# Retention, Mish layer and SwiGLU on one core: moving weight preparation from the retention steps into the slots behind them

## The chip, the cores and the metric

The kernel runs on one core of a Trainium2 chip. The time is the device time of one execution in microseconds, and the smaller it is the better. The kernel before takes 932.82 us (median of 3 runs, 932.62 to 933.05).

## What is computed

Three stages in float32, each feeding the next. The first is retention: causal scores with a decay per head, and no softmax. The second is a two-matrix layer with Mish. The third is a gated layer with SiLU (SwiGLU).

```python
# q, k, v: (4, 8, 576, 64)
scores = scale * q @ k.T ; ret = scores * Dmat      # Dmat[i, j] = gamma[h] ** (i - j), 0 above the diagonal
x = (ret @ v) -> (2304, 512)
h = x @ w_in                                        # (512, 2048)
x = (h * tanh(softplus(h))) @ w_out                 # (2048, 512)
out = (silu(x @ w_gate) * (x @ w_val)) @ w2_out     # 512 -> 1536 -> 512
```

## The kernel before

**Retention** is a list of 20 steps `t`, five for each of the four batches: 128 rows of the sequence each, the fifth of a batch 64 rows. A step has TensorE work (scores `s`, the transposes of k of step t+1 into `tk`, of q ahead of time into `tq`, the state, and the output `o` in two parts, L436 and L443), ScalarE copies (`kT`, `qT`, `sbd`), VectorE work (the mask product `p`, L385, two of them, and the scaled output into `x`, L456) and one GpSimd product `vs`. At its end SP issues the loads of q for step t+4 and of k and v for step t+3. The pools of k and v hold three tiles, so k of step t+3 can only be issued when the state of step t has read k of step t.

**The first layer** is cut into 384 columns of tokens and 16 blocks of 128 hidden units, which makes 96 slots `s` (L577). A slot multiplies block i of the layer's first matrix by x (`g1`, 12 matmuls into a PSUM tile `h`), takes Mish on ScalarE (`m`, L568), splits the result into a high part (ScalarE cast, L573) and a low part (VectorE subtract, L574), together `g`, and multiplies the `g` of four slots earlier by the second matrix (`g2`, 12 matmuls into `acc`, LAG = 4). A slot with i = 0 has `g2` ahead of `g1`. The tiles `h` come from four PSUM banks in turn, so `g1` of slot s+4 overwrites what Mish of slot s has read. Slot 0 stands behind the output of step 17, slot 1 ahead of the output of step 19, slots 2 and on behind retention.

**Weight units.** Both matrices are needed as a high and a low half. There are 32 units of 128 x 1024 words, in the order of `todo` (L67 to L73): four of the first matrix, then one of each in turn. A unit goes through a pipeline, one stage in each call of `weights` (L129): SP fetches it into one of four raw buffers (`fetch`, L83); two calls later ScalarE scales its high words (L103) and VectorE shifts its low ones (L104); one call later VectorE puts in the sign (L108) and joins the words (L112); and then ScalarE copies out the high half (L122) and GpSimd subtracts for the low one (L123), which frees the raw buffer. With `late` set, as in the slots, this last stage waits for the next call. So one call in full flow is one fetch, a scale and a copy on ScalarE, a sign, a shift and a join on VectorE (in this order) and a subtract on GpSimd. Every engine takes its instructions in the order of the program. "Call A" and "call B" below are the first and the second call in a slot. Slot s needs unit 2s - 4 for `g1` and unit 2s - 3 for `g2` (from slot 4 on); a loop in the slot runs further calls if too few are there.

Retention calls the pipeline once in every step (L499), the slots once each until all 32 units are there (L598).

Of the kernel before, what the change touches and what calls it, by code (L numbers as in the profile page):

```python
# [16 lines left out]
def retention_mish_swiglu(  # L17
# [28 lines left out]
    NA, NBU = 19, 13  # L46
# [26 lines left out]
    n1 = len(todo)  # L73
# [9 lines left out]
    def fetch(lim):  # L83
        j = stage[0]
        if j >= min(lim, len(todo)) or j - stage[3] >= RAW:
            return
        stage[0] += 1
        kind, i, src = todo[j]
        raw[j] = xp.tile([128, 2 * DM], U32, tag="raw", name=f"raw{j}", bufs=RAW)
        dst = raw[j] if kind in ("out", "fin") else raw[j].rearrange("p (k f) -> p k f", k=KT)  # L90
        nc.sync.dma_start(out=dst, in_=src)  # L91


    def rebias():
        j = stage[1]
        if j >= stage[0]:
            return
        stage[1] += 1
        rebias_raw(j)
# [6 lines left out]
    def sign(j):  # L106
        lo, hi = words(j)
        nc.vector.scalar_tensor_tensor(lo, hi, 0x80000000, lo, op0=ALU.bitwise_and, op1=ALU.bitwise_or)  # L108

    def join(j):  # L110
        lo, hi = words(j)
        nc.vector.scalar_tensor_tensor(lo, hi, 3, lo, op0=ALU.logical_shift_left, op1=ALU.bitwise_or)  # L112

    def part(lim):
        j = stage[3]
        if j >= min(lim, stage[2]):
            return
        stage[3] += 1
        kind, i, _ = todo[j]
        u = pools["a" if j < NA else "b"].tile([128, 2, DM], F32R, tag="u", name=f"u{j}")  # L120
        w = words(j)[0].bitcast(F32)
        nc.scalar.copy(out=u[:, 0, :], in_=w)  # L122
        nc.gpsimd.tensor_tensor(out=u[:, 1, :], in0=w, in1=u[:, 0, :].bitcast(F32), op=ALU.subtract)  # L123
        unit[kind, i] = u
# [4 lines left out]
    def weights(lim, late=False):  # L129
        j = stage[2]  # L130
        on = j < min(lim, stage[1])
        if on:
            sign(j)
        yield
        if late:
            part(lim)
        if stage[1] < seen[0]:
            rebias()
        seen[:] = seen[1], stage[0]
        yield  # L140
        if on:
            join(j)
            stage[2] += 1
        while not late and stage[3] < stage[2]:
            part(lim)
        fetch(lim + 3)
        seen[1] = stage[0]

    def run(step):
        for _ in step:  # L150
            pass
# [118 lines left out]
    def retention(slot):  # L270
        with ExitStack() as c0:
# [29 lines left out]
            def load(t):  # L301
                if t >= len(steps):
                    return
                b, sc, n = steps[t]
                for nm, src in (("k", k), ("v", v)):
                    x = ld.tile([128, H, D], F32, tag=nm, name=f"{nm}{t}")
                    nc.sync.dma_start(
                        out=x[:n], in_=src[b, :, sc * 128:sc * 128 + n, :].rearrange("h p d -> p h d")
                    )
                    qkv[nm, t] = x  # L310
# [30 lines left out]
            def q_ahead(t, half):  # L341
                b, sc, n = steps[t]
                due = (
                    ((b, 1, 0),) if b else (),
                    ((b, 1, 1),) if b else ((b, 1, 0), (b, 1, 1)),
                    ((b, 2, 0),),
                    ((b + 1, 0, 0),),
                    ((b + 1, 0, 1),),
                )[sc]
                if half < len(due):  # L350
                    q_transposes(*due[half])

            def transposes(t):
                if t >= len(steps):
                    return
                b, sc, n = steps[t]
                src = qkv["k", t]
                p = ps1.tile([128, NP, 128], F32, tag="tk", name=f"tk{t}")
                for pr in range(NP):
                    nc.tensor.transpose(p[:, pr, :n], src[:n, 2 * pr:2 * pr + 2, :], ident[:n, :n])  # L360
                kT[t] = at.tile([128, NP, 128], F32, tag="kT", name=f"kT{t}")
                nc.scalar.copy(out=kT[t][:, :, :n], in_=p[:, :, :n])
                vs[t] = at.tile([128, H, D], F32, tag="vs", name=f"vs{t}")
                nc.gpsimd.tensor_tensor(  # L364
                    out=vs[t][:n],
                    in0=qkv["v", t][:n],
                    in1=gv[:n, sc, :].unsqueeze(2).to_broadcast([n, H, D]),
                    op=ALU.mult,
                )

            def scores(t):
                b, sc, n = steps[t]
                s = [ps1.tile([128, NP, 128], F32, tag=f"s{e}", name=f"s{e}_{t}") for e in range(2)]
                for pr in range(NP):
                    for e in range(2):
                        nc.tensor.matmul(  # L376
                            s[e][:n, pr, :n],
                            lhsT=kT[t][64 * e:64 * e + 64, pr, :n],
                            rhs=q_cols(t)[64 * e:64 * e + 64, pr],
                            start=True,  # L380
                            stop=True,
                        )
                pp[t] = [at.tile([128, NP, 128], F32, tag=f"p{e}", name=f"p{e}_{t}") for e in range(2)]
                for e in range(2):
                    nc.vector.tensor_tensor(  # L385
                        out=pp[t][e][:n, :, :n],
                        in0=s[e][:n, :, :n],
                        in1=mask[:n, :n].unsqueeze(1).to_broadcast([n, NP, n]),
                        op=ALU.mult,
                    )  # L390


            def gout_chunk(sc):
                nc.gpsimd.tensor_tensor(
                    out=gout[:, :, sc * 128:sc * 128 + 128],
                    in0=gout[:, :, :128],
                    in1=gstep[:, :, sc:sc + 1].to_broadcast([128, NP, 128]),
                    op=ALU.mult,
                )
# [3 lines left out]
            def state(t):  # L403
                b, sc, n = steps[t]
                if sc == nsc - 1:
                    return
                if sc == 0:
                    stp[b] = ps1.tile([128, NP, D], F32, tag="st", name=f"state{b}")
                for pr in range(NP):
                    for e in range(2):  # L410
                        h = 2 * pr + e
                        nc.tensor.matmul(  # L412
                            stp[b][64 * e:64 * e + 64, pr, :],
                            lhsT=qkv["k", t][:n, h, :],
                            rhs=vs[t][:n, h, :],
                            start=(sc == 0 and pr == 0),
                            stop=(sc == nsc - 2),
                            skip_group_check=True,
                        )
# [73 lines left out]
            for t in range(len(steps)):  # L493
                scores(t)
                transposes(t + 1)
                q_ahead(t, 0)
                state(t)
                q_ahead(t, 1)
                run(weights(NA))  # L499
                if t + 1 < nsc:  # L500
                    gout_chunk(t + 1)
                if t == len(steps) - 1:
                    slot(1)
                output(t)
                if t == len(steps) - 3:
                    slot(0)
                load_q(t + 4)
                load(t + 3)

    with tc.manual_schedule():  # L510
# [66 lines left out]
        def slot(s):  # L577
            b, i = divmod(s, F1)
            if i == 0 and s:
                g2(s - LAG)  # L580
            g1(s)
            if s >= LAG and i:
                g2(s - LAG)
            d, nm, j = xt, "x", b + 1
            parts = () if b + 1 == NB else (i - F1 + 4,) if b and F1 - 4 <= i < F1 - 2 else range(2, KT) if i == F1 - 1 else ()
            mish(s)
            for kk in parts:
                split_hi(d, nm, j, kk)
            halves(ws.pop(s), s)
            if s < F1 + OFF:  # L590
                while not parts and stage[3] < min(2 * s - OFF + 2 if s > OFF else s, n1):
                    run(weights(n1))
            for kk in parts:
                split_lo(d, nm, j, kk, nc.vector)
            if s >= LAG:
                g2_out(s - LAG)
            if s < F1 + OFF and not parts:
                run(weights(n1, True))  # L598
            second(s)

        retention(slot)
# [282 lines left out]
```

## Time and profile before

| | |
|---|---|
| median of the runs shown | 932.82 us |
| the profiled execution | 934.33 us |
| its span | 932.5 us |
| TensorE busy | 912.3 us, 98% |
| VectorE, ScalarE, GpSimd busy | 520.2, 362.3, 108.6 us |
| granted TensorE clock, mean | 1.00 |

The profiled execution is 1.5 us above the median and 1.8 us above its span. The page of the profile gives busy times and groups of instructions; the stretches show where an engine has idle time; the list of waits shows what ended it; the rows in order of time show what stands behind what. An instruction that is blocked on its engine shows as a longer one.

### The profile page before, as it was taken

The page shows a single profiled execution, that of the slowest core. Times are in us where ns is not written, and L with a number is a line of the kernel's source. Part 1 is how long each engine was busy: PE and PEld are TensorE (multiplying, and loading weights), DVE is VectorE, ACT ScalarE, POOL GpSimd, SP SyncE. Part 2 cuts the span into 40 slices and gives each one's busy share as a digit, 9 for nine tenths or more (in the row PEclk, how much of TensorE's full clock was granted, in tenths as well). Part 3 has the DMA queues.
Part 4 walks back from the last instruction along what each step waited for, and adds up shares of the span by engine and source line. Part 5 has one row for each costly group of instructions (what it writes and reads, how often), then busy time and mean ns, then how long its engine had stood idle before and what let it go on. Part 6 is the DMA issues. An engine that isn't in the chain of part 4 may idle for free.

```text
span 932.5 us, 14692 instructions
## 1 busy us (share of the span) xinstructions
PE 912.3 (98%) x5684; PEld 867.8 (93%) x5684; DVE 520.2 (56%) x929; ACT 362.3 (39%) x731; POOL 108.6 (12%) x90
## 2 busy tenths in 40 slices
PE   8888999999999999999999999999999999999998
PEld 7777899999999999999999999998999998999997
DVE  3897797246556565656535444556544556544444
ACT  4776564345444554545434222223222223222222
POOL 3775344000000000000000000000000000000000
PEclk9999999999999999999999999999999999999999
DMA  9999554035354463554554855544644444644421
GB/s 227 249 236 258 146 152 132 1 113 192 127 185 143 142 201 117 166 182 138 175 180 176 296 203 203 203 158 158 226 158 158 158 158 158 226 158 158 158 69 68
DMA packets 115351, 156.58 MB, mean 168 GB/s; under 512 B 45393, under 2 KB 80977, under 8 KB 115281
## 3 DMA queue, kind: packets, MB, share of 16 engines
q1 hardware_dynamic: 114176, 155.21, 53.4%
q8 instruction: 45, 0.74, 0.4%
q10 hardware_dynamic: 1104, 0.42, 0.2%
q14 instruction: 26, 0.20, 0.1%
HBM read 122.58 MB, written 33.03 MB: 167 GB/s over the span
## 4 chain that ended last, share of the span: by engine, by line
PE 88%; DMA 5%; DVE 3%; ACT 2%; SPq 1%; issue 1%; POOL 0%; ACTq 0%; DVEq 0%; POOLq 0%
PE t L777 28%; PE acc L551 20%; PE h L517 20%; PE fa L703 16%; DMA k<-in_k_dram 4%; PE o L436 1%; PE o L443 1%; DMA rawg<-in_moe_w_gate_dram 1%; PE tk L360 1%; PE s L376 1%; PE state L412 0%; DMA comb<-c 0%; DMA q<-in_q_dram 0%; SPq L91 0%; DVE p L385 0%
## 5 line engine op out<-in xcount | busy, mean ns | idle before, releaser
L777 PE MATMUL t<-y,su 128*128 128x384 f32 x1512 | 306.5, 338 | 1.0 <-DVE cv L744 1.0
L777 PEld LDWEIGHTS t<-y,su 128*128 128x128 f32 x1512 | 271.4, 188 | 24.4 <-DVE cv L744 2.3
L551 PE MATMUL acc<-g,u 128*128 128x384 f32 x1152 | 214.6, 336 | 0.9 <-ACT y L561 0.9
L517 PE MATMUL h<-xs,u 128*128 128x384 f32 x1152 | 214.6, 336 | 0.0
L551 PEld LDWEIGHTS acc<-g,u 128*128 128x128 f32 x1152 | 201.3, 188 | 1.5 <-ACT y L561 1.2
L517 PEld LDWEIGHTS h<-xs,u 128*128 128x128 f32 x1152 | 200.9, 188 | 0.3 <-issue 0.2
L703 PE MATMUL fa<-fu,g 128*128 128x512 f32 x648 | 190.0, 395 | 0.1
L703 PEld LDWEIGHTS fa<-fu,g 128*128 128x128 f32 x648 | 118.6, 188 | 7.5 <-ACT g L725 0.5
L574 DVE TENSOR_TENSOR g<-m,g 128x384 fp32r<-128x384 f32 x96 | 53.6, 558 | 126.8 <-ACT g L573 126.4
L725 ACT CAST g<-sg 128x384 fp32r<-128x384 f32 x72 | 36.9, 513 | 175.0 <-DVE sg L762 121.4
L568 ACT ACTIVATE m<-h 128x384 f32<-128x384 f32 x96 | 47.0, 490 | 145.4 <-PE h L517 144.3
L751 ACT ACTIVATE sg<-sg 128x384 f32<-128x384 f32 x54 | 28.4, 525 | 96.4 <-DVE sg L744 96.4
L730 DVE TENSOR_TENSOR g<-sg,g 128x384 fp32r<-128x384 f32 x72 | 40.2, 558 | 40.6 <-ACT g L725 40.6
L177 POOL TENSOR_TENSOR f<-rawf,f 128x256 fp32r<-128x256 f32 x24 | 23.4, 992 | 284.3 <-ACT f L176 284.3
L123 POOL TENSOR_TENSOR u<-raw,u 128x512 fp32r<-128x512 f32 x32 | 47.1, 1473 | 62.7 <-ACT u L122 61.4
L573 ACT CAST g<-m 128x384 fp32r<-128x384 f32 x96 | 49.3, 514 | 2.6
L744 DVE TENSOR_TENSOR u<-t,p 128x384 f32<-128x384 f32 x36 | 20.1, 557 | 49.8 <-PE t L777 45.6
L744 DVE TENSOR_TENSOR v<-t,p 128x384 f32<-128x384 f32 x36 | 20.0, 556 | 38.1 <-PE t L777 37.4
L104 DVE TENSOR_SCALAR raw<-raw 128x512 uint32<-128x512 uint32 x32 | 36.7, 1146 | 0.0
L762 DVE TENSOR_TENSOR sg<-sg,cv 128x384 f32<-128x384 f32 x54 | 30.2, 559 | 1.9
L122 ACT CAST u<-raw 128x512 fp32r<-128x512 f32 x32 | 21.2, 663 | 20.7 <-DVE raw L112 20.7
L364 POOL TENSOR_TENSOR vs<-v,gv 128x512 f32<-128x512 f32 (+1 forms) x20 | 26.3, 1313 | 22.5 <-DMA v<-in_v_dram 13.2
(79 smaller groups left out, 742.7 us busy)
## 6 DMA issues: line engine op xcount, KB each, us to landing
su<-comb SPq DMA_DIRECT2D x126, 512.0 KB, 3.3
comb<-c SPq DMA_DIRECT2D x84, 256.0 KB, 4.0
raw<-in_moe_w_in_dram SPq DMA_DIRECT2D x16, 512.0 KB, 5.8
raw<-in_moe_w_out_dram SPq DMA_DIRECT2D x16, 512.0 KB, 3.7
rawg<-in_moe_w_gate_dram SPq DMA_DIRECT2D x12, 512.0 KB, 6.5
rawf<-in_moe_w_out_dram SPq DMA_DIRECT2D x12, 512.0 KB, 4.5
rawv<-in_moe_w_val_dram SPq DMA_DIRECT2D x12, 512.0 KB, 6.2
find<-f SPq DMA_DIRECT2D x24, 256.0 KB, 2.4
```

The costliest lines, as they stand in the source:

```text
L104: nc.vector.tensor_scalar(lo, lo, 29, None, op0=ALU.logical_shift_right)
L123: nc.gpsimd.tensor_tensor(out=u[:, 1, :], in0=w, in1=u[:, 0, :].bitcast(F32), op=ALU.subtract)
L517: nc.tensor.matmul(ps, lhsT=u[:, a, kk * 128:(kk + 1) * 128], rhs=s[:, e, :], start=(c == 0), stop=(c == n - 1),)
L551: nc.tensor.matmul(accs[b][d][:, :T], lhsT=u[:, a, d * 128:(d + 1) * 128], rhs=g[:, e, :], start=(i == 0 and c == 0), stop=(i == F1 - 1 an ...
L568: nc.scalar.activation(w, hs.pop(s), AF.Mish)
L573: nc.scalar.copy(out=g[:, 0, :], in_=x)
L574: nc.vector.tensor_tensor(out=g[:, 1, :], in0=x, in1=g[:, 0, :].bitcast(F32), op=ALU.subtract)
L703: nc.tensor.matmul(accs["f", b][m], lhsT=gs[u, e, h][:, x, m * 128:(m + 1) * 128], rhs=fu[2 * (u % PAIRS) + e][:, a, :], start=first, stop ...
L725: nc.scalar.copy(out=gs[u, e, h][:, 0, :], in_=x)
L730: nc.vector.tensor_tensor(out=g[:, 1, :], in0=x, in1=g[:, 0, :].bitcast(F32), op=ALU.subtract)
L744: nc.vector.tensor_tensor(out=out_, in0=a, in1=b_, op=ALU.add)
L777: nc.tensor.matmul(p, lhsT=w[:, n % 2, a, kk * 128:(kk + 1) * 128], rhs=y[:, x, kk, :], start=begin and kk == 0 and (a, x) == (0, 0), stop ...
```

## The change

In retention the call of the pipeline is kept in steps with an odd number only, so there are 10 calls in place of 20. In each slot that still needs units, the call at its end is made twice. Nothing else changes; TensorE's instructions and their order are the same.

```diff
--- before.py
+++ after.py
@@ -496,7 +496,8 @@
                 q_ahead(t, 0)
                 state(t)
                 q_ahead(t, 1)
-                run(weights(NA))
+                if t % 2:
+                    run(weights(NA))
                 if t + 1 < nsc:
                     gout_chunk(t + 1)
                 if t == len(steps) - 1:
@@ -595,7 +596,8 @@
             if s >= LAG:
                 g2_out(s - LAG)
             if s < F1 + OFF and not parts:
-                run(weights(n1, True))
+                for _ in range(2):
+                    run(weights(n1, True))
             second(s)
 
         retention(slot)
```

VectorE, at slot 0 between steps 17 and 18. `x5` is the output of step 17, `g0` the low part of slot 0, `p0_18` and `p1_18` the masked scores of step 18, and the number behind `raw` is that of the unit. Before:

```order
L456 TENSOR_TENSOR x5_1344<-o17_1397,gout_146 128x4x128
L574 TENSOR_TENSOR g0_1428<-m0_1426,g0_1428 128x384
L108 SCALAR_TENSOR_TENSOR raw15_1261<-raw15_1261 128x512
L104 TENSOR_SCALAR raw16_1326<-raw16_1326 128x512
L112 SCALAR_TENSOR_TENSOR raw15_1261<-raw15_1261 128x512
L385 TENSOR_TENSOR p0_18_1447<-s0_18_1437,mask_144 128x512
L385 TENSOR_TENSOR p1_18_1448<-s1_18_1438,mask_144 128x512
```

and now:

```order
L456 TENSOR_TENSOR x5_1263<-o17_1316,gout_146 128x4x128
L575 TENSOR_TENSOR g0_1347<-m0_1345,g0_1347 128x384
L108 SCALAR_TENSOR_TENSOR raw6_1069<-raw6_1069 128x512
L104 TENSOR_SCALAR raw7_1189<-raw7_1189 128x512
L112 SCALAR_TENSOR_TENSOR raw6_1069<-raw6_1069 128x512
L108 SCALAR_TENSOR_TENSOR raw7_1189<-raw7_1189 128x512
L104 TENSOR_SCALAR raw8_1314<-raw8_1314 128x512
L112 SCALAR_TENSOR_TENSOR raw7_1189<-raw7_1189 128x512
L385 TENSOR_TENSOR p0_18_1375<-s0_18_1365,mask_144 128x512
L385 TENSOR_TENSOR p1_18_1376<-s1_18_1366,mask_144 128x512
```

A second sign, shift and join stand between `g0` and the masked scores of step 18, and the units in them are nine lower in number.

VectorE, slots 2 and 3, right behind retention (`g2`, `g3` and `g4` are the low parts of slots 2, 3 and 4). Before:

```order
L574 TENSOR_TENSOR g2_1589<-m2_1587,g2_1589 128x384
L108 SCALAR_TENSOR_TENSOR raw19_1478<-raw19_1478 128x512
L104 TENSOR_SCALAR raw20_1517<-raw20_1517 128x512
L112 SCALAR_TENSOR_TENSOR raw19_1478<-raw19_1478 128x512
L574 TENSOR_TENSOR g3_1616<-m3_1614,g3_1616 128x384
L108 SCALAR_TENSOR_TENSOR raw20_1517<-raw20_1517 128x512
L104 TENSOR_SCALAR raw21_1541<-raw21_1541 128x512
L112 SCALAR_TENSOR_TENSOR raw20_1517<-raw20_1517 128x512
L574 TENSOR_TENSOR g4_1659<-m4_1657,g4_1659 128x384
```

and now:

```order
L575 TENSOR_TENSOR g2_1517<-m2_1515,g2_1517 128x384
L108 SCALAR_TENSOR_TENSOR raw11_1436<-raw11_1436 128x512
L104 TENSOR_SCALAR raw12_1460<-raw12_1460 128x512
L112 SCALAR_TENSOR_TENSOR raw11_1436<-raw11_1436 128x512
L108 SCALAR_TENSOR_TENSOR raw12_1460<-raw12_1460 128x512
L104 TENSOR_SCALAR raw13_1469<-raw13_1469 128x512
L112 SCALAR_TENSOR_TENSOR raw12_1460<-raw12_1460 128x512
L575 TENSOR_TENSOR g3_1553<-m3_1551,g3_1553 128x384
L108 SCALAR_TENSOR_TENSOR raw13_1469<-raw13_1469 128x512
L104 TENSOR_SCALAR raw14_1527<-raw14_1527 128x512
L112 SCALAR_TENSOR_TENSOR raw13_1469<-raw13_1469 128x512
L108 SCALAR_TENSOR_TENSOR raw14_1527<-raw14_1527 128x512
```

Between the low parts of two slots there are six instructions of the pipeline in place of three. This goes on to slot 11; slot 12 has one sign and one join, and from slot 13 on there are none.

SP's queue, from step 9's loads on (the number behind k and v is the step that they are for). Before:

```order
L91 DMA raw9_862<-in_moe_w_out_dram 128x1024
L307 DMA k12_878<-in_k_dram 128x8x64
L307 DMA v12_880<-in_v_dram 128x8x64
L91 DMA raw10_929<-in_moe_w_in_dram 128x4x256
L298 DMA q14_944<-in_q_dram 64x8x64
L307 DMA k13_946<-in_k_dram 128x8x64
L307 DMA v13_948<-in_v_dram 128x8x64
L91 DMA raw11_995<-in_moe_w_out_dram 128x1024
L292 DMA q15_1013<-in_q_dram 128x8x128
```

and now:

```order
L307 DMA k12_833<-in_k_dram 128x8x64
L307 DMA v12_835<-in_v_dram 128x8x64
L298 DMA q14_890<-in_q_dram 64x8x64
L307 DMA k13_892<-in_k_dram 128x8x64
L307 DMA v13_894<-in_v_dram 128x8x64
L91 DMA raw5_941<-in_moe_w_out_dram 128x1024
L292 DMA q15_959<-in_q_dram 128x8x128
L307 DMA k14_961<-in_k_dram 64x8x64
L307 DMA v14_963<-in_v_dram 64x8x64
```

A fetch stands in every second step only, and the loads behind steps 8, 10, 12 and so on follow one another with no fetch between.

## Rows read from the trace of the kernel before

**Rows 1.** Page, part 1: busy us (share of the span) x instructions.

```profile
PE 912.3 (98%) x5684; PEld 867.8 (93%) x5684; DVE 520.2 (56%) x929; ACT 362.3 (39%) x731; POOL 108.6 (12%) x90
```

**Rows 2.** Stretches: steps 2 to 17; retention's end to slot 16.

```profile
core 0: us, PE busy (x) PEld busy (x) DVE busy (x) ACT busy (x) POOL busy (x), PEclk, DMA share, GB/s
...
19.46:99.31 79.85, 70.10 (x954) 60.08 (x953) 68.03 (x96) 55.61 (x107) 50.86 (x38) 1.00 1.05 247
...
111.47:165.86 54.39, 54.39 (x317) 54.39 (x314) 44.63 (x59) 31.47 (x59) 22.50 (x14) 1.00 0.44 136
```

**Rows 3.** Waits, 19.46 to 99.31: us in total, times, longest.

```profile
PE tk L360 <- DMA k<-in_k_dram: 7.4, 7, 2.0
...
PE state L412 <- ACT sbd L426: 1.7, 2, 1.1
...
PE o L443 <- DVE p L385: 0.4, 2, 0.2
```

**Rows 4.** Waits of SP's queue, the same stretch.

```profile
SPq L91 <- POOL u L123: 10.3, 7, 3.2
```

**Rows 5.** Order of time, slot 0 to step 18: start, us, engine, line, instruction.

```profile
103.24 0.69 DVE L108 SCALAR_TENSOR_TENSOR raw<-raw 128x512 uint32<-128x512 uint32 x1
...
103.84 0.42 DVE L104 TENSOR_SCALAR raw<-raw 128x512 uint32<-128x512 uint32 x1
104.18 0.68 DVE L112 SCALAR_TENSOR_TENSOR raw<-raw 128x512 uint32<-128x512 uint32 x1
104.78 1.28 DVE L385 TENSOR_TENSOR p<-s,mask 128x512 f32<-128x512 f32 x2
...
105.52 0.43 PE L443 MATMUL o<-p,vs 128*64 128x128 f32 x2 [0.83 <-DVE p L385]
105.63 1.29 POOL L123 TENSOR_TENSOR u<-raw,u 128x512 fp32r<-128x512 f32 x1 [3.36 <-ACT u L122]
```

**Rows 6.** Order of time, one slot with one call.

```profile
122.25 0.68 DVE L112 SCALAR_TENSOR_TENSOR raw<-raw 128x512 uint32<-128x512 uint32 x1
122.85 0.55 DVE L574 TENSOR_TENSOR g<-m,g 128x384 fp32r<-128x384 f32 x1
122.96 0.66 ACT L122 CAST u<-raw 128x512 fp32r<-128x512 f32 x1 [0.97 <-DVE raw L112]
123.31 0.68 DVE L108 SCALAR_TENSOR_TENSOR raw<-raw 128x512 uint32<-128x512 uint32 x1
...
123.70 1.48 POOL L123 TENSOR_TENSOR u<-raw,u 128x512 fp32r<-128x512 f32 x1 [1.66 <-ACT u L122]
...
123.92 1.54 DVE L104 TENSOR_SCALAR raw<-raw 128x512 uint32<-128x512 uint32 x1
...
124.61 0.52 ACT L573 CAST g<-m 128x384 fp32r<-128x384 f32 x1
...
125.38 0.68 DVE L112 SCALAR_TENSOR_TENSOR raw<-raw 128x512 uint32<-128x512 uint32 x1
```

**Rows 7.** VectorE and GpSimd in order of time, where a join meets a GpSimd product.

```profile
62.67 0.68 DVE L112 SCALAR_TENSOR_TENSOR raw<-raw 128x512 uint32<-128x512 uint32 x1
62.69 1.56 POOL L364 TENSOR_TENSOR vs<-v,gv 128x512 f32<-128x512 f32 x1 [0.83 <-PE tk L360]
...
87.26 0.42 DVE L104 TENSOR_SCALAR raw<-raw 128x512 uint32<-128x512 uint32 x1
87.27 1.30 POOL L364 TENSOR_TENSOR vs<-v,gv 128x512 f32<-128x512 f32 x1 [0.48 <-DMA v<-in_v_dram]
...
87.59 1.53 DVE L112 SCALAR_TENSOR_TENSOR raw<-raw 128x512 uint32<-128x512 uint32 x1
```

**Rows 8.** VectorE in order of time: the low part of slot 2.

```profile
116.58 0.54 DVE L574 TENSOR_TENSOR g<-m,g 128x384 fp32r<-128x384 f32 x1
```

**Rows 9.** Chain that ended last: the last product of slot 15 and the first of slot 16.

```profile
163.78 4.16 PE acc L551 x24
```

**Rows 10.** DMA issues, 118 to 136 us: count, KB each, median us to landing.

```profile
raw<-in_moe_w_in_dram SPq DMA_DIRECT2D x3, 512.0 KB, 3.7
```

## The prediction

> **What bounds the kernel now.** The page comes first: TensorE is busy for 98% of the span [rows 1], so a change counts only where it takes TensorE's idle time away or makes new. The stretches say where that idle time is [rows 2]. In steps 2 to 17 TensorE works 70.10 of 79.85 us. From 111.47 (the start of slot 2; I call it R, the end of retention) to 165.86 (the start of slot 16) it works all of 54.39 us. So there is something to win in retention, 9.75 us, and in the slots only something to lose. The list of waits names the 9.75 us [rows 3]: 7.4 for k from memory, 1.7 for ScalarE's copy of the state behind a copy of the pipeline, 0.4 for a mask product: 9.5. The DMA engines are full there, a share of 1.05 at 247 GB/s [rows 2], and SP stands 10.3 us before fetches until GpSimd frees a raw buffer, with the next loads of k and v queued behind [rows 4]. TensorE's order does not change, so the sum has three terms: what retention wins, what slot 0 costs it, and the idle time that the slots get.
>
> **Term 1, half of retention's calls go.** Up to step 17 there are 9 fetches in place of 18. That is 9 x 0.52 = 4.7 MB of 79.85 us x 247 GB/s = 19.7 MB [rows 2]. The other 15.0 MB take 61 us at this rate, less than TensorE's 70.10, so memory no longer sets the pace. Behind even steps no fetch stands before the loads, and a raw buffer is free long before its next fetch. VectorE and ScalarE lose a sign, shift, join, scale and copy in these steps, GpSimd a subtract; they ran beside TensorE and count only through the 2.1 us of waits for them. Of the 9.5 us I take 8.2 as gone: the loads of k that follow half a megabyte of q, and one wait for the state's copy in an odd step, may keep about 1.3. The ends are half of it, 4.8, and all of it, 9.5.
>
> **How VectorE and GpSimd meet.** This sets the other two terms. A free shift takes 0.42 us and a free sign or join 0.68 [rows 5]. One that comes while a GpSimd instruction runs ends only behind it: the shift at 123.92 takes 1.54 and ends 0.28 after the subtract [rows 6], the join at 87.59 takes 1.53 and ends 0.55 after the product. Who comes first wins: the join at 62.67, 0.02 ahead of the product, takes its 0.68, and the product is the longer one, 1.56 against 1.30 [rows 7].
>
> **Term 2, the second call in slot 0.** It stands ahead of step 18's mask products, for which TensorE waits already (0.83) [rows 5]. Its sign takes the place of the product, at 104.78. By the spacing of the same three rows the shift follows 0.60 later and the join would start 0.34 after that, at 105.72. The subtract comes at 105.63, under the shift, and goes first, as at 87.27 [rows 7]; it runs from about 105.69 for 1.29, and the join ends 0.55 later, at 107.53. Without the call VectorE was free at 104.86. So the products come 2.7 us later, and so does all of TensorE's work up to R. With the join first it would be 0.60 + 0.34 + 0.60 = 1.5.
>
> **Term 3, two calls in slots 2 to 11.** One slot with one call [rows 6], from join to join: the join ends at 122.93, the copy starts 0.03 later, the subtract at 123.70 and ends at 125.18, the shift ends at 125.46, the next join at 126.06: 3.13 us, a closed loop over three engines, in which the low part (0.55) and the sign are hidden. Call A is this same loop, 3.13. In call B no low part stands ahead. With a for the end of A's join, the sign starts at a - 0.08, the shift at a + 0.52, and the join would at a + 0.86. The subtract of the unit joined by A comes at a + 0.77 (122.93 to 123.70), 0.09 sooner. It runs from the shift's end, a + 0.83, to a + 2.13, and the join ends at a + 2.68. So a slot takes 3.13 + 2.68 = 5.8 us on this loop, against TensorE's 4.16 (two products in 4.16) [rows 9]. ScalarE needs less, so its added scales and copies are hidden there. A fetch goes out when B's subtract frees a buffer, at a + 2.13, and lands 3.7 us later [rows 10], at a + 5.8; the shift of the next slot's B wants it at a + 5.8 + 0.5. That fits with half a us to spare, and SP holds nothing else back, only further fetches.
>
> TensorE has a lead of four slots, and this is what hides the loop at first. The low part of slot 2 ends at 117.12 now, R + 5.65 [rows 8]. With a call more before it and one less ahead of step 19's products I put R + 6.1; the bounds are 5.1 and 8.3. Ten slots on, the low part of slot 12 ends at R + 6.1 + 58.1 = R + 64.2. Slot 16 opens with the product that reads it, at R + 54.4 [rows 2, 9]. So TensorE stands 9.8 us in sum. It begins about slot 11 or 12, where `g1` waits for a PSUM bank that Mish of four slots before has not read yet, with some 1.65 us a slot. From slot 13 on no calls are left and the low parts follow their products; nothing later has idle time that could give the loss back.
>
> **Sum.** -8.2 + 2.7 + 9.8 = +4.3 us. The profiled execution's 934.33 becomes 938.6, its span 936.8. The median of the runs shown is 1.5 lower: 932.8 + 4.3 = **937.1 us**. With term 1 between 9.5 and 4.8 this case goes from 935.8 to 940.5.
>
> **Rivals.**
> *Call B's join gets in first.* It misses by 0.09 us by my spacing, and a copy that starts late would turn it. Then ScalarE's order sets the loop: from a copy's start to the end of its cast 2.17 us [rows 6], then the low part and sign (about 1.1), the subtract 1.29, 0.28 for the shift and 0.60 for the join: about 5.45. Slot 12's low part ends at R + 5.1 + 54.5 = R + 59.6, an idle time of 5.2, and slot 0 costs 1.5: -8.2 + 1.5 + 5.2 = -1.5, 931.3 us (930.0 to 934.7 with term 1's ends).
> The Trainium skill (SBUF — State Buffer, section Who interferes with whom) says that VectorE instructions with two SBUF inputs share a port pair with GpSimd, that the first to start keeps it for the whole instruction, and that the order of issue decides. By that rule alone either order is possible, 937.1 or 931.3; the rows at 87.27 are what makes me choose.
> *The lead is never used up: faster.* If the two engines met less than rows 6 show, a slot would be 0.55 + 2 x 1.54 = 3.6 us of VectorE, under 4.16, and TensorE would not stand at all: -8.2 + 1.5 = -6.7, 926.1 us. It decides at about 4.85 us a slot, where slot 12 is just in time. Against it: the single loop is 3.13, so call B would have to do with 1.7.
> *Everything blocks.* Call B as long as A, 6.26 a slot, the late start R + 8.3, and half of term 1: -4.8 + 2.7 + (8.3 + 62.6 - 54.4 = 16.5) = +14.4, 947.2 us. A fetch that lands late would do the same.
> *The clock.* The wait ahead of step 18's output grows from 0.83 to 3.5 us; the longest now is 2.0 [rows 3], and the granted clock stays at 1.00, its level of 2.4 GHz [rows 2]. If it fell to 1.2 GHz behind this wait, the 5.9 us of work from 105.52 to R could take twice as long: up to 943.0 us.
> The Trainium skill (TensorE: The Clock Gate, section HAM oscillation — how this bites in real kernels) warns of long idle gaps for this reason; no row here shows a lower clock.
>
> **How the numbers follow.** The forecast gets 0.52, the join first 0.22, the lead that holds 0.12, everything blocked 0.09, the clock 0.05. 930.0 to 943.0 leaves out the third and most of the fourth, 0.2. Faster by over 0.2% (1.9 us, about what a measurement of this kernel can tell from no change) are the third case and a third of the second, 0.20; within 0.2% the rest of the second and the edge of the forecast, 0.16; slower 0.64.
>
> **What would show it.** Right: waits for k in steps 2 to 17 near 1 us; R near 106 (111.47 - 8.2 + 2.7); a wait of some 3.5 us ahead of step 18's output; in slots 2 to 11 low parts 5.8 us apart and a join in call B of about 1.8 us; TensorE idle from slot 11 or 12 to 16, most of it just ahead of slot 16, 9.8 in sum; nothing new behind. Wrong: joins of 0.68 in call B; no idle time in the slots; R later than 109; a granted clock under 1.00.

## The result, and the profile after

The changed kernel takes **943.07 us** (median of 4 runs, 942.04 to 944.71) against 932.93 of the kernel before (4 runs, 932.62 to 933.8): a ratio of 1.0112, with an interval of 1.0096 to 1.0127. It is slower by 10.1 us, where 4.3 were forecast, and just outside the range. The profiled execution took 942.04 us with a span of 940.3, against 934.33 and 932.5 before: the two traces account for 7.8 us of it. The rest is spread between executions, the profiled one of before being 1.4 above the 932.93 and the one of after 1.0 below the 943.07.

The page's first part (busy us, share of the span, instructions) answers to [rows 1]:

```profile
PE 915.6 (97%) x5684; PEld 869.8 (93%) x5684; DVE 514.2 (55%) x929; ACT 361.6 (38%) x731; POOL 99.9 (11%) x90
```

TensorE has the same 5684 instructions and is busy for longer: some of them ran slower. The stretches, cut as in [rows 2], say where (us, busy time of each engine, granted clock, DMA):

```profile
core 0: us, PE busy (x) PEld busy (x) DVE busy (x) ACT busy (x) POOL busy (x), PEclk, DMA share, GB/s
19.53:87.87 68.34, 68.12 (x955) 59.50 (x953) 39.84 (x69) 43.98 (x89) 31.16 (x29) 1.00 0.99 226
87.87:104.17 16.30, 12.67 (x127) 11.27 (x125) 9.60 (x16) 6.95 (x15) 6.08 (x5) 0.90 0.30 98
104.17:167.22 63.05, 55.83 (x315) 53.91 (x312) 62.07 (x78) 37.06 (x66) 30.60 (x22) 1.00 0.55 175
167.22:180.28 13.06, 8.48 (x36) 7.92 (x37) 6.56 (x10) 5.72 (x12) 2.76 (x2) 0.87 0.13 41
```

The four are steps 2 to 17; slot 0 to R; R to the start of slot 16; the start of slot 16 over its two products and the first of slot 17. Before, the first took 79.85 us [rows 2], and the other three these:

```profile
99.31:111.47 12.16, 11.17 (x126) 9.95 (x124) 9.40 (x15) 5.74 (x13) 5.26 (x4) 1.00 0.34 109
111.47:165.70 54.23, 54.23 (x316) 54.23 (x313) 44.47 (x59) 31.47 (x59) 22.50 (x14) 1.00 0.44 136
165.70:171.95 6.25, 6.25 (x37) 6.25 (x37) 1.93 (x4) 1.56 (x3) 0.21 (x1) 1.00 0.01 3
```

[rows 2] ends the third at 165.86, which is the end of the matmul ahead of slot 16; slot 16's own first matmul starts at 165.70, as its counterpart after does at 167.22.

| stretch | before | after | difference | forecast |
|---|---|---|---|---|
| steps 2 to 17 | 79.85 | 68.34 | -11.51 | -8.2 |
| slot 0 to R | 12.16 | 16.30 | +4.14 | +2.7 |
| R to slot 16 | 54.23 | 63.05 | +8.82 | +9.8 |
| slot 16 and behind it | 6.25 | 13.06 | +6.81 | 0 |
| the rest | | | -0.46 | 0 |
| span | 932.5 | 940.3 | +7.8 | +4.3 |

The list of waits of TensorE from 15 to 185 us (us in total, times, longest) begins with five lines. [rows 3], which ends ahead of slot 0, has only the second of them, at 0.4 us:

```profile
PE h L518 <- ACT m L569: 5.3, 4, 1.4
PE o L443 <- DVE p L385: 3.6, 2, 3.5
PE h L518 <- ACT xs L252: 3.1, 1, 3.1
PE acc L552 <- ACT g L574: 1.9, 1, 1.9
PE h L518 <- DVE xs L257: 1.4, 1, 1.4
```

No wait for `k` is left in steps 2 to 17, and 0.2 us of waits for the state's copy. `m` and `g` are the slots' (Mish's bank, and the high part that slot 16's first product reads); `p` is the mask product of step 18; `xs`, the split of `x` for block 1, was in no step of the prediction.

**Step 18**, in order of time (start, us, engine, line, instruction), answers to [rows 5]:

```profile
94.21 1.30 POOL L123 TENSOR_TENSOR u<-raw,u 128x512 fp32r<-128x512 f32 x1 [5.01 <-ACT u L122]
94.28 1.78 DVE L112 SCALAR_TENSOR_TENSOR raw<-raw 128x512 uint32<-128x512 uint32 x1
...
95.98 1.27 DVE L385 TENSOR_TENSOR p<-s,mask 128x512 f32<-128x512 f32 x2
...
96.71 0.43 PE L443 MATMUL o<-p,vs 128*64 128x128 f32 x2 [3.46 <-DVE p L385]
...
97.31 1.97 PE L443 MATMUL o<-p,vs 128*64 128x128 f32 x14 [0.17 <-DVE p L385]
```

The subtract gets in ahead of the join, the join takes 1.78 in place of 0.68, and TensorE waits 3.46 us, 2.63 more than before. Behind the wait the 14 products take 1.97 us. Before, they took 1.09:

```profile
106.12 1.09 PE L443 MATMUL o<-p,vs 128*64 128x128 f32 x14 [0.16 <-DVE p L385]
```

A window of 2 us in the changed kernel shows why (same columns as the stretches):

```profile
97.50:99.50 2.00, 2.00 (x20) 1.67 (x20) 0.18 (x1) 0.00 (x0) 0.72 (x1) 0.50 0.76 208
```

The granted clock stands at 0.50 of full speed, 1.2 GHz, for some 3 us, and is back at 1.00 before 101. From the output of step 18 to R it is 7.46 us (96.71 to 104.17) against 5.95 before: 1.51 for the clock, which with 2.63 makes the 4.14.

**A slot with two calls**, VectorE and GpSimd, from low part (L575) to low part:

```profile
109.60 0.54 DVE L575 TENSOR_TENSOR g<-m,g 128x384 fp32r<-128x384 f32 x1
...
110.67 1.53 DVE L104 TENSOR_SCALAR raw<-raw 128x512 uint32<-128x512 uint32 x1
...
113.59 1.34 POOL L123 TENSOR_TENSOR u<-raw,u 128x512 fp32r<-128x512 f32 x1 [1.67 <-ACT u L122]
113.66 1.82 DVE L112 SCALAR_TENSOR_TENSOR raw<-raw 128x512 uint32<-128x512 uint32 x1
...
115.40 0.55 DVE L575 TENSOR_TENSOR g<-m,g 128x384 fp32r<-128x384 f32 x1
```

115.40 - 109.60 = 5.80 us. Call A's shift is the blocked one (1.53), call B's join the other (1.82), and the subtract came 0.07 us ahead of it. The low part of slot 12 ends at 168.06, R + 63.9. The five waits ahead of slots 12 to 16 are 7.2 us of the 8.82; the other 1.6 is what TensorE loses where it starts again (from 143.51 to 149.31 it is 5.80 us: two products of 2.08 and a wait of 1.36 leave 0.28).

**Slot 16**, TensorE, answers to [rows 9]:

```profile
167.22 2.38 PE L552 MATMUL acc<-g,u 128*128 128x384 f32 x12 [1.88 <-ACT g L574]
169.44 1.21 PE L518 MATMUL h<-xs,u 128*128 128x384 f32 x6
173.77 0.44 PE L518 MATMUL h<-xs,u 128*128 128x384 f32 x1 [3.13 <-ACT xs L252]
175.65 4.79 PE L518 MATMUL h<-xs,u 128*128 128x384 f32 x17 [1.44 <-DVE xs L257]
```

The first product of block 1 (from 169.44) gets through 6 of its 12 matmuls and stops. It needs the last two pieces of the split of `x`, which slot 15 puts on ScalarE (L252, high parts) and VectorE (L257, low parts); the 17 matmuls of the last row are its own 5 and slot 17's 12. ScalarE, and then VectorE:

```profile
172.84 0.48 ACT L569 ACTIVATE m<-h 128x384 f32<-128x384 f32 x1
173.22 0.91 ACT L252 CAST xs<-x 128x384 fp32r<-128x384 f32 x2
```

```profile
174.57 0.56 DVE L575 TENSOR_TENSOR g<-m,g 128x384 fp32r<-128x384 f32 x1 [1.05 <-ACT g L574]
175.05 1.02 DVE L257 TENSOR_TENSOR xs<-x,xs 128x384 fp32r<-128x384 f32 x2
```

Both stand behind the Mish, casts and low parts of slots 13 to 15, which the loop has made late. Before, the same two instructions were these, ScalarE's and VectorE's, and the product that reads them began at 167.79:

```profile
164.21 0.92 ACT L252 CAST xs<-x 128x384 fp32r<-128x384 f32 x2
```

```profile
166.05 1.02 DVE L257 TENSOR_TENSOR xs<-x,xs 128x384 fp32r<-128x384 f32 x2
```

The first of the two low pieces was there at 166.56 (half of 1.02), and the eighth matmul, which reads it, came at 167.79 + 7 x 0.173 = 169.0: some 2.4 us to spare. The low part of slot 12 was there at 152.97, 12.7 us ahead of the product that reads it, at 165.70. So the lead of four slots is that of the low parts `g` and does not hold for the split. The 17 matmuls behind the waits take 4.79 us; in experiment 10 the same 17 take 3.23, at a granted clock of 1.00. Waits 4.57, clock 1.56, and 0.7 lost where TensorE starts again: 6.8 us.

### The profile page after: what moved, and what is told of

It reads as the page before. It is cut to its first block, busy times and chain, and to the rows that moved or that the text cites. A ratio compares the mean times of both kernels' runs of the same rounds, so it can differ in the third digit from the quotient of the medians.

```text
span 940.3 us, 14715 instructions
## 1 busy us (share of the span) xinstructions
PE 915.6 (97%) x5684; PEld 869.8 (93%) x5684; DVE 514.2 (55%) x929; ACT 361.6 (38%) x731; POOL 99.9 (11%) x90
## 4 chain that ended last, share of the span: by engine, by line
PE 86%; issue 4%; POOL 3%; DVE 3%; DMA 2%; ACT 1%; SPq 0%; POOLq 0%; DVEq 0%; ACTq 0%
PE t L779 28%; PE acc L552 18%; PE h L518 18%; PE fa L705 15%; POOL u L123 3%; PE s L376 2%; PE o L443 1%; PE o L436 1%; PE tk L360 1%; DMA k<-in_k_dram 1%; DMA raw<-in_moe_w_out_dram 1%; PE state L412 1%; DVE raw L112 1%; PE tq L329 1%; DMA q<-in_q_dram 0%
## 5 line engine op out<-in xcount | busy, mean ns | idle before, releaser
L518 PE MATMUL h<-xs,u 128*128 128x384 f32 x1152 | 217.5, 338 | 9.9 <-ACT m L569 5.3
L575 DVE TENSOR_TENSOR g<-m,g 128x384 fp32r<-128x384 f32 x96 | 54.1, 563 | 120.3 <-ACT g L574 119.9
L123 POOL TENSOR_TENSOR u<-raw,u 128x512 fp32r<-128x512 f32 x32 | 44.5, 1392 | 63.3 <-ACT u L122 58.8
L112 DVE SCALAR_TENSOR_TENSOR raw<-raw 128x512 uint32<-128x512 uint32 x32 | 35.1, 1096 | 0.0
L456 DVE TENSOR_TENSOR x<-o,gout 128x512 f32<-128x512 f32 (+1 forms) x22 | 12.9, 592 | 31.6 <-PE o L443 31.6
```

Source lines behind the costliest of these rows:

```text
L518: nc.tensor.matmul(ps, lhsT=u[:, a, kk * 128:(kk + 1) * 128], rhs=s[:, e, :], start=(c == 0), stop=(c == n - 1),)
L575: nc.vector.tensor_tensor(out=g[:, 1, :], in0=x, in1=g[:, 0, :].bitcast(F32), op=ALU.subtract)
```

## The experiments

The first four stood beside 13 runs of the kernel before (median 933.27), the next four beside 17 (933.06), the last two beside 15 (932.91). All diffs are against the changed kernel.

### 1. Slot 0's second call goes to step 18

```diff
-                if t % 2:
+                if t % 2 or t == len(steps) - 2:
                     run(weights(NA))
...
-                for _ in range(2):
+                for _ in range(2 if s else 1):
                     run(weights(n1, True))
```

> The second call of slot 0 runs in step 18 instead, behind that step's mask products; the number of calls up to slot 1 is the same. First theory (from slot 2 on the loop of ScalarE, GpSimd and VectorE sets the time, and slot 0's call counts only as far as it delays the start of that loop): the wait ahead of step 18's output falls from 3.5 to about 0.8 us, no lower clock there, slot 2 starts 4.1 us earlier, but the low part of slot 2 ends only about 1.8 us earlier, and so does the kernel: about 941.2. Second theory (slot 0's call is on the path in full): 4.1 us faster, about 939.

941.44 us (940.21 to 942.41), 1.6 less than the changed kernel's 943.07; the ranges of the two sets of four runs just overlap. TensorE around step 18:

```profile
94.18 0.43 PE L443 MATMUL o<-p,vs 128*64 128x128 f32 x2 [0.83 <-DVE p L385]
94.78 1.09 PE L443 MATMUL o<-p,vs 128*64 128x128 f32 x14 [0.17 <-DVE p L385]
```

The wait is 0.83 again, the 14 products take 1.09 us, and R comes at 100.15, 4.0 us sooner. But slot 16 opens at 165.52, only 1.7 sooner. So term 2 and its clock loss come from the second call of slot 0, and of the 4.0 us the loop behind takes 2.3 back: once TensorE waits for the loop, an earlier R is worth little.

### 2. The split of block 1 goes to retention

```diff
-    NA, NBU = 19, 13
-    RAW, XS = 4, 6
+    NA, NBU = 18, 14
+    RAW, XS = 4, 8
...
-            parts = () if b + 1 == NB else (i - F1 + 4,) if b and F1 - 4 <= i < F1 - 2 else range(2, KT) if i == F1 - 1 else ()
+            parts = () if b + 1 == NB else (i - F1 + 4,) if b and F1 - 4 <= i < F1 - 2 else range(2, KT) if b and i == F1 - 1 else ()
...
-        pools["c"] = cr.enter_context(tc.tile_pool(name="pc", bufs=4, side="right"))
+        pools["c"] = cr.enter_context(tc.tile_pool(name="pc", bufs=2, side="right"))
...
-        SA, SB = 4, 5
+        SA, SB = 2, 7
```

> The last two quarters of x of the second block are split in retention instead of in slot 15 (two more buffers for them; the pools of units, of the third layer's weights and of the second stage's outputs are cut differently to make room). First theory (slot 16 waits 4.6 us because slot 15's split stands behind the late Mish and casts on ScalarE, and the clock falls behind that wait): both waits of slot 16's first product go, no lower clock there, slot 16 to slot 17's second product takes about 6.3 us and not 13.1, the kernel is 6 to 7 us faster, about 936. Second theory (everything on ScalarE and VectorE is late there, the split is only the last in line): the wait moves to the Mish of slots 13 to 15 and less than 2 us are won.

961.58 us, a total that says nothing of the split: the two more tiles of the split are paid for with other buffers. Among the waits from 185 to 520 us:

```profile
ACT c L176 <- DMA comb<-c: 97.0, 46, 5.5
```

In the changed kernel this wait is 14.7 us. ScalarE waits for stores with two `pc` buffers in place of four, and TensorE, which waits 1.0 us in all from 185 us on in the changed kernel, waits 19.6 here. What can be read is slot 16:

```profile
167.81 3.92 PE L552 MATMUL acc<-g,u 128*128 128x384 f32 x12 [1.87 <-ACT g L574]
171.56 4.33 PE L518 MATMUL h<-xs,u 128*128 128x384 f32 x24
175.72 2.27 PE L552 MATMUL acc<-g,u 128*128 128x384 f32 x12
```

The wait for `g` is the same 1.87, both waits for `xs` are gone, and the 24 matmuls of slot 16's and slot 17's products run through. From slot 16's start over three products it is 7.91 us against 13.06, with a lower clock in the first (3.92). So those waits are the late split; the 6 to 7 us that were expected of the whole kernel can't be read from this run.

### 3. The low half's subtract goes to VectorE in the slots

```diff
-    def part(lim):
+    def part(lim, dve=False):
...
-        nc.gpsimd.tensor_tensor(out=u[:, 1, :], in0=w, in1=u[:, 0, :].bitcast(F32), op=ALU.subtract)
+        (nc.vector if dve else nc.gpsimd).tensor_tensor(out=u[:, 1, :], in0=w, in1=u[:, 0, :].bitcast(F32), op=ALU.subtract)
...
         if late:
-            part(lim)
+            part(lim, True)
```

> The subtract for a unit's low half runs on VectorE in the slots, so GpSimd does nothing there. First theory (blocked signs, shifts and joins make the slot 5.8 us): shifts 0.42 and joins 0.68 throughout, a slot takes 4.9 to 5.4 us though VectorE has more to do, slot 16 opens 4 to 9 us earlier against slot 2, and the kernel takes 932 to 939. Second theory (the chain of copy, scale, Mish and cast on ScalarE sets 5.8): the slot stays at 5.8 us or grows by the added 2 x 0.7.

934.5 us (932.47 to 936.37, 10 runs), 8.6 less than the changed kernel, and a ratio to before of 1.0012 (1.0000 to 1.0024). VectorE in one slot:

```profile
114.00 0.55 DVE L575 TENSOR_TENSOR g<-m,g 128x384 fp32r<-128x384 f32 x1
...
115.07 0.69 DVE L123 TENSOR_TENSOR u<-raw,u 128x512 fp32r<-128x512 f32 x1
115.67 0.42 DVE L104 TENSOR_SCALAR raw<-raw 128x512 uint32<-128x512 uint32 x1
116.01 0.69 DVE L112 SCALAR_TENSOR_TENSOR raw<-raw 128x512 uint32<-128x512 uint32 x1
...
119.00 0.55 DVE L575 TENSOR_TENSOR g<-m,g 128x384 fp32r<-128x384 f32 x1
```

VectorE has two instructions more in a slot, every shift is back at 0.42 and every join at 0.69, and a slot takes 5.0 to 5.3 us in place of 5.80. R to slot 16 is 56.36 us (103.70 to 160.06). So what made the slots 5.8 us long is how VectorE and GpSimd block one another, as term 3 had it, and not VectorE's own work.

### 4. Work for TensorE in the gap ahead of step 18's output

```diff
+                if t == len(steps) - 2:
+                    fill = ps1.tile([128, NP, 128], F32, tag="tq", name="fill")
+                    for _ in range(22):
+                        nc.tensor.matmul(fill[:, 0, :], lhsT=ident, rhs=ident, start=True, stop=True)
```

> 22 matmuls that nobody reads fill the wait ahead of step 18's output. First theory (the 3.5 us without work lower the clock to 1.2 GHz, and this delays slot 2 and the loop that starts there): the granted clock stays 1.00 up to slot 2, the second part of that output takes 1.1 us and not 2.0, slot 2 starts about 1.4 us earlier, and the kernel is about 1.4 us faster. Second theory (VectorE's and ScalarE's queues are the later ones there anyway): slot 2 starts earlier, the kernel's time does not change.

941.85 us (941.4 to 942.83), 1.2 less than the changed kernel, with ranges that overlap. TensorE, where the fill stands in the gap:

```profile
93.05 5.08 PE L443 MATMUL fill<-ident 128*128 128x128 f32 x44
98.05 1.09 PE L447 MATMUL o<-p,vs 128*64 128x128 f32 x16
```

The fill, not the mask product, holds step 18's output now, at 98.05 in place of 96.71 (in this execution the join of 94.24 took its 0.69 us, though the subtract's recorded start, 94.20, is the earlier one, and the mask product was done at 96.12). Even so R comes 0.7 us sooner (103.45), with a clock of 1.00 from 93 us to R. So the lower clock in that place follows from TensorE's idle time and not from what else runs there. Slot 16 opens at 167.29, 0.07 later than without the fill: again the loop takes what is won ahead of it.

### 5. The transfers of retention without their units

```diff
+            dm = cp.tile([128, 3, 256], U32, tag="dm", name="dm")
...
                 if t % 2:
                     run(weights(NA))
+                elif t < 18:
+                    nc.sync.dma_start(out=dm, in_=cols(w1_in, t % F1)[:, :3])
```

> The changed kernel, with a transfer of the size of a unit's fetch (393 KB) issued by SP in each even step up to 16, into a tile that nothing reads; VectorE, ScalarE and GpSimd do nothing for it. It asks why steps 2 to 17 became 11.5 us shorter. First theory (the transfers of the units make k's land late, and TensorE waits for k): the transfers are back to one a step, so at least two thirds of the 11.5 us are lost again, the stretch from step 2 to step 17 takes 76 to 80 us with waits of ScalarE and TensorE for k, k's transfers take 5.5 us or more from issue to landing, and the time is 950 to 952 us, if the slots stay as they are. Rival (VectorE, ScalarE and GpSimd were what the steps waited for, and the calls that left freed them): the stretch stays at 68 to 70 us, k's waits stay under 1 us in all, and the time is 942 to 945 us.

The transfer is three quarters of a unit's fetch, 393 of 524 KB, and not all of it.

948.83 us (947.45 to 951.09), 5.8 more than the changed kernel; the profiled execution is the slowest of the four. Steps 2 to 17, and TensorE's waits in them:

```profile
19.49:96.59 77.10, 71.85 (x954) 62.40 (x952) 40.31 (x69) 43.87 (x89) 31.76 (x29) 0.96 1.08 243
```

```profile
PE tk L361 <- DMA k<-in_k_dram: 5.2, 5, 1.9
```

VectorE, ScalarE and GpSimd do what they do in the changed kernel (40, 44, 32 us) and 8.76 of the 11.51 us are lost. `k` lands after a median of 5.8 us, as before the change, where the changed kernel has 4.8. Of the 8.76, 5.2 are waits for `k`; the other 3.6 go with a lower clock behind two of them (below), which the kernel before did not have. SP stands 2.0 us before fetches, not the 10.3 of [rows 4], so the transfers by themselves bring the waits back. So most of term 1 is the memory's; how much of the rest is SP's queue or the engines is not shown.

### 6. A smaller dose: three steps

```diff
-                if t % 2:
+                if t not in (3, 8, 13):
...
-                for _ in range(2):
+                for _ in range(2 if s in (2, 4, 6) else 1):
```

> A smaller dose of the same change: the call is left out in steps 3, 8 and 13 alone, and made up by second calls in slots 2, 4 and 6. First theory (the loss is a backlog of VectorE and GpSimd that lasts up to slot 15 and makes the split of x late; with three second calls it is made up for by slot 12): no wait of TensorE for a split of x in slot 16, no product waits for a unit in slots 2 to 16 by more than 1 us, the wait ahead of step 18's output is 0.8 us as before the change, and retention keeps a third to a half of its 11.5 us: 927 to 930 us. Rival (a second call in a slot costs its price wherever it stands, by about 1 us each, on TensorE's path): 930 to 933 us.

930.19 us (927.57 to 931.43), a ratio to before of 0.9960 (0.9946 to 0.9975). Retention is 3.8 us shorter (76.04), slot 0 to R takes 12.17 as before, and from 95 to 185 us the only waits of TensorE are the two ahead of step 18's output, 1.0 in sum. A second call in a slot costs nothing where the slots behind make it up; the median is at the border of the two theories' ranges, the missing waits are the first one's.

### 7. Experiments 1 and 3 together

> Two edits together: the low half's subtraction of the units that are finished in the slots goes to VectorE, and slot 0's second call goes to step 18. First theory (the loop over the slots remains the bound up to slot 16, and the call in step 18 moves its start by less than it moves the output of step 18): slot 16 opens 1.7 us sooner than with the first edit alone, and the time is 1 to 3 us less than that kernel's 934.5 us: 931.5 to 933.5 us. Rival (with the shorter loop the products no longer wait for it, so what the move gives ahead of step 18's output is kept in full, the lower clock there included): 4 us less or more, 928 to 930.5 us.

932.97 us (932.04 to 935.65, 11 runs), within the first theory's range, and the rival's 4 us are excluded. Its path is not shown, though: in the profiled execution, the slowest of the eleven, slot 16 opens at 160.71, 0.65 later than in experiment 3, and 3.8 us of waits for the split are still there. The two edits don't add up.

### 8. Six steps, and the low half on VectorE

```diff
-                if t % 2:
+                if t not in (3, 5, 8, 10, 13, 15):
...
-                for _ in range(2):
+                for _ in range(2 if s in (2, 3, 4, 5, 6, 7) else 1):
```

and the edit of experiment 3.

> The call is left out in steps 3, 5, 8, 10, 13 and 15, made up by second calls in slots 2 to 7, and the low half's subtraction of the units that are finished in the slots is VectorE's. First theory (a second call now costs VectorE 5.15 us a slot against some 4.2 us of TensorE; the six slots with two calls fall behind by some 6 us, the lead of four slots covers it, and slots 8 to 14 with one call make it up ahead of slot 15's split): no product waits for a unit by more than 1 us, none for a split of x in slot 16, clock at its full level in the slots; retention keeps 7 to 10 us of its 11.5: 923 to 927 us. Rival (the backlog reaches slot 15 all the same, so that the split of x stands behind it): waits of 2 us or more for the split of x in slot 16 and a lower clock behind them, 928 to 932 us.

**925.20 us** (924.08 to 927.29), a ratio to before of 0.9913 (0.9900 to 0.9926): 7.9 us faster than the kernel before, 17.9 than the changed one. The stretch of steps 2 to 17, and all waits of TensorE from 95 to 185 us:

```profile
19.41:91.48 72.07, 69.89 (x955) 60.89 (x953) 45.70 (x78) 47.88 (x95) 35.39 (x32) 0.98 1.00 232
```

```profile
PE o L443 <- DVE p L385: 1.0, 2, 0.8
```

Slot 0 to R takes 12.17 us, as before. What retention wins (7.8) is what the kernel wins; the slots give nothing back.

### 9. The same with the low half on GpSimd

> The last kernel with one edit undone: the call is left out in the same six steps and made up in slots 2 to 7, but the low half's subtraction is GpSimd's again, so a slot with two calls takes the loop 5.8 us and one with a single call 3.13. First theory (split of x in slot 15 is the first thing to be late): the low part of slot 2 at R + 5.7, of slot 8 at R + 40.5, of slot 15 at R + 62.4 in place of R + 59.7; no product waits for a unit or a bank by more than 1 us, but TensorE waits in slot 16 for the split of x, 1 to 3 us in all, perhaps with a lower clock behind it: 1 to 4 us more than the kernel with the low half on VectorE, 926.5 to 929 us. Rival (the lead of four slots covers the split too): no wait in the slots, within 1 us of that kernel's 925.2. Second rival (the products are late first): waits for Mish's bank or for g from slot 10 to 12 on, 929 us or more.

932.01 us (929.8 to 933.2, 11 runs), 6.8 more than experiment 8. The low parts come where the loop puts them: slot 8's ends at R + 40.45 (40.5 expected), slot 15's at R + 62.1 (62.4). TensorE:

```profile
141.76 2.36 PE L518 MATMUL h<-xs,u 128*128 128x384 f32 x12 [1.28 <-ACT m L569]
...
163.07 0.44 PE L518 MATMUL h<-xs,u 128*128 128x384 f32 x1 [1.26 <-ACT xs L252]
165.31 4.79 PE L518 MATMUL h<-xs,u 128*128 128x384 f32 x17 [1.80 <-DVE xs L257]
```

Both the first theory and the second rival are seen: the split comes 3.06 us late, at the edge of the first theory's 1 to 3, and the clock falls behind it, but ahead of it stands the rival's wait for Mish's bank, in slot 12 (1.28). The median is 3 us above the first theory's range and in the rival's. By the trace the split is the larger part: its waits and the clock's 1.56, which was not priced, are 4.6 of the 6.8. Its R + 59.7 for an undisturbed slot 15 was wrong too: in the trace of before that low part ends at 166.13, R + 54.7.

### 10. Eight steps, and the low half on VectorE

```diff
-                if t % 2:
+                if t not in (2, 4, 6, 8, 10, 12, 14, 16):
...
-                for _ in range(2):
+                for _ in range(2 if s in (2, 3, 4, 5, 6, 7, 8, 9) else 1):
```

and the edit of experiment 3.

> As the kernel with six steps and the low half on VectorE, but the call is left out in eight steps (2, 4, up to 16) and made up in slots 2 to 9. First theory (retention gives back about 1.3 us for each call that is left out; a slot with two calls takes VectorE 5.0 us and one with a single call 2.6, against 4.16 of TensorE, so eight slots fall 6.7 us behind and slots 10 to 14 make up 7.7): steps 2 to 17 some 10 us shorter than before, no wait of 1 us or more in the slots: 921.5 to 924 us. Rival (what is made up comes too late for slot 15's split of x): 1.5 us or more of waits in slot 16 and a lower clock behind them, 925 to 928 us.

925.23 us (923.92 to 926.05), the same as experiment 8. Retention is 10.4 us shorter (69.43), and one wait is back in slot 16:

```profile
160.52 3.23 PE L518 MATMUL h<-xs,u 128*128 128x384 f32 x17 [1.44 <-DVE xs L257]
```

It lies between the two theories: the rival's wait, without the lower clock. Of the 2.6 us that retention gains over experiment 8, 2.0 go into this wait and the start behind it; the profiled spans are 0.7 apart, and the medians, equal, do not show even that.

## Why the prediction was wrong

**What held.** The slots are slower by the mechanism that term 3 gives. Call B's join loses to the subtract (by 0.07 us, 0.09 forecast), a slot takes 5.80 us, slot 2's low part ends at R + 6.0 (6.1), slot 12's at R + 63.9 (64.2), TensorE's waits begin in slot 12 (143.51, 1.27 us for Mish's bank), and the longest of them stands ahead of slot 16 (1.88 of 7.20, not most of it). The 8.82 measured are less than 9.8 mainly because that product starts on the high part, which is there 0.9 us before the low one; the forecast also had slot 16 at R + 54.4 before, where it is R + 54.2. Experiment 3 shows the cause, and rules out that VectorE's added work alone is the bound. The order at call B was a near thing: in experiment 4, at step 18, the join won with a recorded start 0.04 us behind the subtract's. In term 2 the wait of 3.5 us came as forecast, and with it +2.63 of the +2.7; experiment 1 shows that the second call makes it.

**The step that failed** is the end of term 3: from slot 13 on "the low parts follow their products", so that the lead of four slots covers what is late and nothing is lost behind the opening of slot 16 ("nothing new behind"). What else stands behind the late low parts is put at nothing, without a reason. The lead is that of the low parts alone. Slot 15 also puts the split of `x` for block 1 behind the late low parts, and slot 16 reads it at once. That cost 6.8 us, 4.57 of it waits (experiment 2: gone when the split is elsewhere; experiment 9: there when slot 15 is late; experiment 8: not there when it is on time). The trace of before would have shown it: 2.4 us to spare, where the loop was forecast to be some 10 late.

**The clock** stood as a rival of its own with 0.05, to be taken in place of the forecast. It came on top of it, in two places: 1.5 us behind step 18 (of the 5.9 that the rival allowed) and 1.56 behind the split. That the time lies 0.1 us from this rival's 943.0 is chance: the lower clock cost 3.1 us in two places, not 5.9 in one. The Trainium skill (TensorE: Matmul & The Clock Gate, section HAM oscillation — how this bites in real kernels) warns of a lower clock behind long idle gaps. This trace agrees, with 0.50 behind the wait of 3.46 us; the last section has shorter waits with a lower clock behind them. A cost that adds to the likeliest case belongs in its sum.

**Term 1** was mis-sized the other way: -11.5 against -8.2, outside its ends of -4.8 and -9.5. The direction was right, and by experiment 5 most of the cause. Its cap was TensorE's idle time, 9.75 us [rows 2]. But the busy 70.10 us of before were no floor: in the changed kernel, with hardly a wait left, the same work is 68.12. That the 2 us were a cost of the waits is read from this difference, not tested. Its 9 fetches are 8 in this stretch (16 before, 8 after: 19.72 and 15.43 MB), which changes nothing in the argument.

The errors, less time with a minus: -3.3 in term 1, +1.4 in slot 0, -1.0 in term 3, +6.8 behind it, -0.5 in the rest, which takes the forecast +4.3 to +7.8 in the spans. The last 2.3 us of the 10.1 are between executions. That the sum is only 3.5 us off is luck: the gain that term 1 missed hides half of the split's loss.

## What to carry to other kernels

When work is moved out of a stretch that waits into one that is full, follow every instruction that stands behind it on its engine up to the first reader with the smallest slack, not only the tiles that are moved: here the low part of slot 12 had 12.7 us of lead and the split in slot 15 had 2.4. Move as much as the engine there can make up before that reader, and see what slows it first: six of the ten calls moved, with one subtract on another engine, gave 7.9 us where all ten cost 10.1. A long wait of TensorE can cost more than its length: here the lower clock behind two of them added some 1.5 us each.

## What the runs showed of the hardware

**The clock behind a wait** cost some 1.5 us in each of the two places of the changed kernel, but the wait's length alone does not tell whether it falls. In experiment 5 the clock fell behind waits of 1.88 and 1.47 us in retention; windows of 2 us behind each:

```profile
52.00:54.00 2.00, 2.00 (x18) 1.89 (x12) 0.00 (x0) 0.90 (x2) 0.41 (x1) 0.55 0.99 182
...
76.00:78.00 2.00, 2.00 (x21) 1.88 (x22) 0.34 (x1) 1.97 (x4) 1.24 (x1) 0.52 0.71 164
```

In the kernel before, a wait of 2.03 us for `k` (to 77.20) was followed by 1.00, and so was the one of 1.44 in experiment 10. The wait ahead of slot 16 shows both: behind its 1.88 us in the changed kernel the product takes 2.38, behind 1.87 in experiment 2 it takes 3.92. What decides stays open.

**Moving an instruction to the busier engine shortened its loop.** GpSimd's subtract takes 1.30 to 1.80 us and stretches a shift from 0.42 to 1.53 or a join from 0.68 to 1.82; on VectorE it takes 0.69. VectorE gains by doing it itself: 5.0 to 5.3 us a slot in place of 5.80.
